# Narrower idle matmuls, separate PSUM banks for the first three visits, and a first layer that takes its first tokens in halves

## The chip, the core and the metric

The kernel runs on one core of one Trainium2 chip. The metric is the device time of one execution in microseconds (us), taken as the median of several runs; lower is better.

## What is computed

Sliding-window causal attention, followed by a two-layer network with a silu between its layers:

```python
q, k, v: (8 batches, 8 heads, 576 positions, 64), float32
scores = q @ k.T / 8, where 0 <= i - j < 64, else -1e9
attn = softmax(scores) @ v
x = attn.transpose(0, 2, 1, 3).reshape(4608, 512)      # tokens x model
out = silu(x @ w_in) @ w_out                           # w_in 512x2048, w_out 2048x512
```

## The kernel before, in words

**Attention.** The 4608 tokens are 72 blocks of 64, nine to a batch. Because of the window, a block needs its own keys and those of the block before it. A *visit* is 3 blocks (the first four visits) or 4. A visit runs through these steps: `scores` (L286) on TensorE, small matmuls of 32 rows and 64 columns into four PSUM banks (for the first batch, four matmuls at L293 first write the mask as a bias); `expo` (L306) on ScalarE; `masking` on VectorE (not in the first batch); `values` (L326) on TensorE; then on VectorE `inverse` (L338), `normal` (L342), which divides and frees the banks of `values`, and `cross` (L350), which transposes the result into `bridge`, where the network reads it. q and k arrive by DMA, and VectorE turns them (L283, L281). v arrives by DMA in groups of 128 positions, and copies of its halves (L264) go to VectorE or ScalarE.

**Network.** The tokens are nine tiles of 512. The first layer (`first_layer`, L361) makes, for each of 16 *ff tiles* of 128 rows, four matmuls (one for each 128 model columns) into one PSUM bank, and `silu` (L367) on ScalarE brings them to SBUF. Tile 0 is taken in parts: for four ff tiles at a time the first 384 tokens (visits 0 and 1), or the next 192 (visit 2). The second layer of tile 0 (`second_layer`, L371) keeps four banks open, one for each 128 tokens, and goes through the ff tiles, so it has 64 matmuls of 512 columns, and each pair of ff tiles needs one of eight loads of `w_out` (L271). `copy_out` (L376) then copies the four banks to SBUF, on VectorE or ScalarE. Tiles 3 to 8 use a scheme with seven products in place of eight (L397).

**Order.** A planner (`Plan`, L16) writes the order of each engine's instructions in advance: it plays the kernel through with an estimated time for each step (`us`), its dependences, the PSUM banks from named pools, and ranks, and then emits the instructions in the order that it found. On the chip each engine keeps that order, and semaphores enforce the dependences. What the planner believes of times changes only the order. Pool `at0` gives the first visits' scores banks 0-3 or 4-7, `two` gives their values banks 0-1 or 2-3, `mp` gives the network banks 4-7 until the attention is done.

**Idle matmuls.** Until there is work, TensorE multiplies zeros (`warm`, L677). They are fillers of the lowest rank: L726 and L727 put matmuls of 256 columns ahead of the first scores, and L728 puts matmuls of 512 columns wherever TensorE would idle between the first scores and the first layer. They write to a bank of pool `any`.

**DMAs.** All loads but the first rows of q and k are issued by GpSimd (POOL), in a fixed order, with up to eight in flight: v and rows of the first batch, eight loads of `w_in` (two for four ff tiles), three of `w_out`, then rows and v of the second batch with the other five of `w_out` in between (L708 to L722), then the other batches.

Of the kernel before, what the change touches and what calls it, by code (L numbers as in the profile page):

```python
# [15 lines left out]
class Plan:  # L16
# [13 lines left out]
    def add(self, cls, us, fn, deps=(), lat=0.1, gate=None, dma=None, pool=None, table=None, first=None, slow=0.0):  # L30
        op = dict(us=us, first=self.rank[cls] if first is None else first, fn=fn, deps=[d for d in deps if d is not None],
                  lat=lat, gate=gate, dma=dma, pool=pool, table=table, seen=None, n=self.count, until=[], bank=None, cls=cls, slow=slow)
        self.count += 1
        self.queues.setdefault(cls, []).append(op)
        return op
# [13 lines left out]
    def run(self):  # L49
# [7 lines left out]
        mode = "full"  # L57
        events, order = [0.7], []
        while left:
# [6 lines left out]
            while moved:  # L66
                moved = False
                for e in engines:
# [58 lines left out]
def kernel(ctx, tc, q, k, v, w_in, w_out, out):  # L127
# [56 lines left out]
        rank=dict(one=-9, late=6, dma=-1, ldk=-9, ldq=-9, cast0=-5,  st=-2, vs=-3, silu=-3, out=-2, keep=-2.1, ssum=-1.2, tsum=1.2,  # L184
                  s=1, v=0, moe=99, warm=200, warm2=200, exp=1, mask=1, inverse=0, norm=0.1, cross=0.2, turn=-1.25, cast=-4,
# [175 lines left out]
    def first_layer(bank, j, ft, c, lo, hi):  # L361
        n0 = j * TB % NBR
        nc.tensor.matmul(  # L363
            ps[:, bank["bank"][0], 0:hi - lo], lhsT=w_in_sb[:, c, ft * 128:(ft + 1) * 128],
            rhs=bridge[:, n0 + lo // 64:n0 + hi // 64, c // 2, :, c % 2], start=(c == 0), stop=(c == NDC - 1))
# [123 lines left out]
    o_done = {}  # L489
    e_free, ob_free, ob_ring = {}, {}, {}  # L490
# [23 lines left out]
    def add_visit(vi):  # L514
# [11 lines left out]
        vi["s"] = s  # L526
        ex = p.add("exp" + z, {"ACT": 0.19 + 0.00084 * 256 * ns}, lambda _: expo(s, vi), [s], table="exp")
# [4 lines left out]
        pv = p.add("v" + z, {"PE": 0.05 * ns + 0.1}, None, [ma] + need_v(vi), pool="two" if vi["banks"] == 2 else "at",  # L532
                   gate=(lambda: moe[20][0]["seen"] is not None) if i == 2 else None)
        pv["fn"] = lambda _: values(pv, vi)
        e_free[i] = [pv]
        rc = p.add("inverse" + z, {"DVE": 0.28}, lambda _: inverse(pv, vi), [pv] + ob_free.get(i - NOB, []))
        no = p.add("norm" + z, {"DVE": 0.16 + 0.00107 * 128 * ns}, lambda _: normal(pv, vi), [rc] + ob_free.get(i - NOB, []))
# [3 lines left out]
        ob_free[i] = [cr]  # L541
        for n in range(vi["n0"], vi["n0"] + vi["nb"]):
            o_done[n] = cr
# [15 lines left out]
    def add_part(j, fts, gt, lo, hi, left):  # L559
# [15 lines left out]
        for n in blocks:  # L575
            br_free[n] = [moe[-1][0]]

# [237 lines left out]
```

## Time and profile before

| | |
|---|---|
| median of 3 runs | 294.48 us |
| lowest and highest | 294.23 and 295.61 us |
| the profiled execution's own time | 294.13 us |
| its span in the profile | 292.4 us |
| first matmul of the first layer | at 23.27 us |
| first matmul of tile 0's second layer | at 40.18 us |
| first matmul of tile 1's first layer | at 56.21 us |

All times inside the profile are counted from the span's start, and come from one execution; 1.7 us of its time lie outside the span. A row of the timeline has the start, the duration, the engine, the line, the operation, what it writes and reads, its shape, the count, and in brackets the idle time before it and what ended that. PE is TensorE's matmuls, PEld its weight loads, DVE VectorE, ACT ScalarE. A row of a window has busy time and count for each engine, the granted clock, the mean busy share of the DMA engines, and GB/s; DMA shares over 1 mean packets that overlap. A row of DMA issues ends in the median time from issue to landing, in us; a row of a DMA queue has packets, MB, and the share of 16 engines' time. A few matmul records are missing from the trace.

### The profile page before, as it was taken

The numbers are of one execution on the slowest core, as the hardware profiler recorded it, in microseconds if no ns is written. First come the engines' busy times: TensorE is split into PE (matmuls) and PEld (weight loads), VectorE is DVE, ScalarE is ACT, GpSimd is POOL, SyncE is SP. The second block draws the span as 40 slices with busy tenths as digits, with TensorE's granted clock in tenths as the row PEclk, the third lists the DMA queues.
The fourth block names the chain that finished last, engine by engine and source line by source line (L and its number), as shares of the span: only waits on it lengthen the run. The fifth ranks groups of instructions, "written<-read, shape, count | busy, mean of one in ns | idle before, by whom it ended". The sixth has DMA issues, their size and how long they took to land.

```text
span 292.4 us, 9098 instructions
## 1 busy us (share of the span) xinstructions
PE 282.0 (96%) x3957; PEld 181.3 (62%) x3971; DVE 163.9 (56%) x303; ACT 164.8 (56%) x255; POOL 117.8 (40%) x181
## 2 busy tenths in 40 slices
PE   8959999999999999999999999999999999999995
PEld 6735764597444455447854686478647864784584
DVE  3663237591580168755987697469446944422433
ACT  2647782798528763668276744673567356416610
POOL 8784597897776988789900000000000000000000
PEclk9999999999999999999999999999999999999999
DMA  9999999999999999999997003000300030003013
GB/s 147 125 166 199 177 134 175 154 215 149 164 189 194 107 192 175 209 154 138 118 165 193 2 4 141 5 2 4 143 0 2 6 144 4 0 2 143 0 38 108
DMA packets 89000, 32.05 MB, mean 110 GB/s; under 512 B 75904, under 2 KB 84096, under 8 KB 88960
## 3 DMA queue, kind: packets, MB, share of 16 engines
q0 software_dynamic: 81600, 18.00, 68.0%
q1 hardware_dynamic: 6176, 12.29, 13.3%
q10 hardware_dynamic: 1184, 1.18, 1.3%
q8 instruction: 31, 0.51, 0.7%
q14 instruction: 9, 0.07, 0.1%
HBM read 36.70 MB, written 9.44 MB: 158 GB/s over the span
## 4 chain that ended last, share of the span: by engine, by line
PE 95%; issue 2%; DVE 1%; ACT 1%
PE ps L363 42%; PE ps L404 26%; PE ps L372 14%; PE ps L678 5%; PE ps L334 4%; PE ps L301 4%; DVE ob L345 1%; PE ps L293 0%; ACT ot L377 0%; ACT L369 0%; DVE ot L416 0%; ACT g L369 0%; DVE rc L340 0%; DVE idle L222 0%
## 5 line engine op out<-in xcount | busy, mean ns | idle before, releaser
L363 PE MATMUL ps<-bridge,w_in_sb 128*128 128x512 bf16 (+3 forms) x704 | 127.0, 340 | 0.8 <-DVE ot L377 0.4
L369 ACT ACTIVATE g<-ps 128x512 bf16<-128x512 f32 (+3 forms) x176 | 89.8, 520 | 43.7 <-PE ps L363 42.6
L363 PEld LDWEIGHTS <-w_in_sb 128*128 128x128 bf16 x704 | 66.8, 98 | 57.9 <-issue 1.0
L395 DVE TENSOR_TENSOR gsum<-g 128x512 bf16<-128x512 bf16 x48 | 20.1, 419 | 44.7 <-ACT g L369 44.7
L372 PE MATMUL ps<-w_out_sb,g 128*128 128x512 bf16 x178 | 41.1, 379 | 1.7 <-issue 1.6
L308 ACT ACTIVATE e<-ps 128x2048 bf16<-128x2048 f32 (+1 forms) x19 | 34.0, 1787 | 13.6 <-PE ps L301 13.5
L404 PEld LDWEIGHTS <-gsum 128*128 128x128 bf16 x384 | 37.1, 98 | 4.5
L404 PE MATMUL ps<-g,gsum 128*128 128x256 bf16 x288 | 36.4, 273 | 0.0
L231 POOL DMA_DIRECT2D natk<-in_k_dram x48 | 28.9, 617 | 12.2 <-DMA natk<-in_k_dram 3.6
L372 PEld LDWEIGHTS <-g 128*128 128x128 bf16 x192 | 17.7, 98 | 20.2
L231 POOL DMA_DIRECT2D natq<-in_q_dram x48 | 29.0, 623 | 2.9 <-DMA vo<-in_v_dram 1.2
L317 DVE TENSOR_TENSOR e<-e,mask 128x2048 bf16<-128x2048 bf16 (+1 forms) x16 | 19.2, 1201 | 19.1 <-ACT e L308 18.9
L404 PEld LDWEIGHTS <-g 128*128 128x128 bf16 x288 | 27.3, 98 | 4.0
L242 POOL DMA_DIRECT2D vo<-in_v_dram x32 | 28.6, 907 | 2.7 <-PE ps L334 1.1
L407 ACT COPY part<-ps 128x256 f32<-128x256 f32 x23 | 8.6, 372 | 30.2 <-PE ps L404 27.1
L404 PE MATMUL ps<-w_out_sb,g 128*128 128x256 bf16 x192 | 23.0, 273 | 0.0
L353 DVE STREAM_TRANSPOSE bridge<-ob 128x1024 bf16<-128x1024 bf16 (+1 forms) x19 | 22.1, 1172 | 0.3
L345 DVE TENSOR_TENSOR ob<-ps,rc 128x1024 bf16<-128x1024 f32 (+1 forms) x19 | 21.9, 1158 | 0.4
L416 DVE TENSOR_TENSOR ot<-ps,part 128x256 f32<-128x256 f32 (+1 forms) x30 | 13.8, 469 | 9.1 <-PE ps L404 4.7
L678 PE MATMUL ps<-idle 128*128 128x256 bf16 (+1 forms) x87 | 14.7, 334 | 4.4 <-issue 3.0
L281 DVE STREAM_TRANSPOSE qt<-natq 128x576 uint32<-128x576 uint32 x12 | 9.1, 759 | 14.5 <-PE ps L301 14.5
L377 ACT COPY ot<-ps 128x512 f32<-128x512 f32 x10 | 5.8, 586 | 16.8 <-PE ps L372 12.8
(56 smaller groups left out, 223.4 us busy)
## 6 DMA issues: line engine op xcount, KB each, us to landing
out_dram<-ot SPq DMA_DIRECT2D x32, 256.0 KB, 3.6
vo<-in_v_dram POOLq DMA_DIRECT2D x32, 128.0 KB, 6.1
natq<-in_q_dram POOLq DMA_DIRECT2D x48, 72.0 KB, 5.4
natk<-in_k_dram POOLq DMA_DIRECT2D x48, 72.0 KB, 4.0
ve<-vo SPq DMA_DIRECT2D x12, 264.0 KB, 4.8
w_in_sb<-in_moe_w_in_dram POOLq DMA_DIRECT2D x8, 256.0 KB, 8.3
w_out_sb<-in_moe_w_out_dram POOLq DMA_DIRECT2D x8, 256.0 KB, 7.3
natq<-in_q_dram POOLq DMA_DIRECT2D x10, 96.0 KB, 6.0
```

The costliest lines, as they stand in the source:

```text
L231: nc.gpsimd.dma_start(out=nats[kk][b % NK][r, h // 4].rearrange("p c x -> p (c x)").rearrange("p (t x) -> p t x", x=2 * D), in_=(q, k)[kk] ...
L242: nc.gpsimd.dma_start(out=vos[b % NV][:, g, :, 0:D], in_=v[b, :, 128 * g:128 * g + 128].rearrange("h p d -> p h d"))
L308: nc.scalar.activation(out=es[vi["i"] % NES][:, :, 0:ns].rearrange("p j s i -> p j (s i)"), in_=ps[:, op["bank"][0]:op["bank"][0] + 4, 0:6 ...
L317: nc.vector.tensor_mul(e, e, m)
L345: nc.vector.tensor_mul(obs[vi["i"] % NOB][:, 0:4 * vi["nb"]].rearrange("p s (i x) -> p (s i) x", i=2).rearrange("p (b k) x -> p b k x", b= ...
L353: nc.vector.transpose(out=br.rearrange("p n Q u h i -> p (n Q u h) i"), in_=ob.rearrange("p s (h d) -> p (s h) d", h=2))
L363: nc.tensor.matmul(ps[:, bank["bank"][0], 0:hi - lo], lhsT=w_in_sb[:, c, ft * 128:(ft + 1) * 128], rhs=bridge[:, n0 + lo // 64:n0 + hi // ...
L369: nc.scalar.activation(out=g[:, lo:hi], in_=ps[:, bank["bank"][0], 0:hi - lo], func=ACTF.Silu)
L372: nc.tensor.matmul(ps[:, bank["bank"][0]], lhsT=gall[:, slot, m * 128:(m + 1) * 128], rhs=w_out_sb[:, f], start=(f == 0), stop=(f == NFT - 1))
L395: (nc.vector.tensor_sub if i else nc.vector.tensor_add)(out=t[i], in0=a, in1=b)
L404: nc.tensor.matmul(ps[:, bank["bank"][0], lo:lo + 256], lhsT=lhs, rhs=rhs, start=first, stop=last, skip_group_check=True)
L678: nc.tensor.matmul(ps[:, op["bank"][0], 0:128 * op["parts"]], lhsT=idle, rhs=idle.unsqueeze(1).to_broadcast([128, op["parts"], 128]), star ...
```

## The change

It has three parts, and estimates of the planner that go with them.

1. The idle matmuls before the first scores have 128 columns instead of 256. By the order built, 96 of them stand there, then 13 of 512 columns (before: 68 of 256); two of 512 stand between the first and the second scores (before: three), none between the first and second values (before: five), and nine between the second values and the third scores (before: two there, and nine behind the third scores).
2. The banks: scores of the first three visits in 0-3, 4-7 and 2-5, their values in 2-3, 0-1 and 2-3. The values of the first two visits now stand directly behind one another, and the third scores stand behind both. On VectorE the first visit's transpose is forced ahead of the second visit's normalization.
3. For the first four ff tiles, `add_halves` takes the 384 tokens as 2 x 192: first all four ff tiles with the first visit's tokens, in banks 6, 7, 0 and 1, then all four with the second visit's, into the other columns of the same banks. One silu of 384 columns follows for each.

The planner also counts TensorE instructions (`code`) and adds a delay at instructions 449, 705 and so on. This alters no instruction, only its idea of when steps can start.

```diff
         mode = "full"
+        code, chunk = 0, {449: 0.0}
...
+                        for x in range(193, code + op["code"], 256):
+                            if x >= code:
+                                t = us * (x - code) / op["code"]
+                                us += max(0.0, chunk.get(x, 0.0) - now - t)
+                                chunk[x + 256] = max(now + t, chunk.get(x, 0.0)) + (5.6 if now < 25 else 2.5)
+                        code += op["code"]
...
-        {"at": lambda: [(0, 1, 2, 3)], "at0": lambda: [(0, 1, 2, 3), (4, 5, 6, 7)], "any": lambda: [(3,), (2,), (7,), (6,)],
-         "two": lambda: [(0, 1), (2, 3)],
+        {"at": lambda: [(0, 1, 2, 3)], "at0": lambda: [(0, 1, 2, 3)], "at1": lambda: [(4, 5, 6, 7)], "at2": lambda: [(2, 3, 4, 5)], "any": lambda: [(3,), (2,), (7,), (6,)],
+         "two0": lambda: [(2, 3)], "two1": lambda: [(0, 1)], "mp0": lambda: [(6,), (7,), (0,), (1,)],
...
-    def first_layer(bank, j, ft, c, lo, hi):
+    def first_layer(bank, j, ft, c, lo, hi, at=0):
...
-            ps[:, bank["bank"][0], 0:hi - lo], lhsT=w_in_sb[:, c, ft * 128:(ft + 1) * 128],
-            rhs=bridge[:, n0 + lo // 64:n0 + hi // 64, c // 2, :, c % 2], start=(c == 0), stop=(c == NDC - 1))
+            ps[:, bank["bank"][0], at:at + hi - lo], lhsT=w_in_sb[:, c, ft * 128:(ft + 1) * 128],
+            rhs=bridge[:, n0 + lo // 64:n0 + hi // 64, c // 2, :, c % 2], start=(c == 0 and at == 0), stop=(c == NDC - 1),
+            skip_group_check=True)
...
-        vi["banks"] = 2 if first else 4
+        vi["banks"] = 2 if i < 3 else 4
...
-                  gate=None if first else gate_scores(vi), pool="at0" if vi["n0"] < 9 else "at")
+                  gate=None if first else gate_scores(vi), pool=("at0", "at1", "at2")[i] if first else "at")
...
-        no = p.add("norm" + z, {"DVE": 0.16 + 0.00107 * 128 * ns}, lambda _: normal(pv, vi), [rc] + ob_free.get(i - NOB, []))
+        no = p.add("norm" + z, {"DVE": 0.16 + 0.00107 * 128 * ns}, lambda _: normal(pv, vi), [rc] + ob_free.get(i - NOB, []) + (cr0 if i == 1 else []))
...
+    def add_halves(fts, gt):
+        first = {}
+        for i in range(2):
+            for ft in fts:
+                for c in range(NDC):
+                    op = p.add("moe", {"PE": 0.0036 + 192 / 2400}, None, [o_done[3 * i], win[(ft, c)]], pool=None if c or i else "mp0")
+                    bank = first.setdefault(ft, op)
+                    op["fn"] = lambda _, bank=bank, ft=ft, c=c, i=i: first_layer(bank, 0, ft, c, 192 * i, 192 * i + 192, 192 * i)
+                    moe.append((op, 1, 1 if c == 0 and i == 0 else -1, 0))
+                if i:
+                    slot, si = gt[ft]
+                    op = p.add("silu", {"ACT": 0.18 + 384 * 0.00083}, lambda _, bank=bank, slot=slot: silu(bank, slot, 0, 384), [op], table="silu")
+                    si.append(op)
+                    bank["until"] = [op]
...
-    p.add_filler(26, "warm", {"PE": 0.214}, warm, 2, [c_idle], pool="any", lat=0.0)
-    p.add_filler(60, "warm", {"PE": 0.109}, warm, 2, [c_idle], gate=lambda: visits[0]["s"]["seen"] is None, pool="any", lat=0.0)
-    p.add_filler(60, "warm2", {"PE": 0.217}, warm, 4, [c_idle], pool="any", lat=0.0,
-                 gate=lambda: visits[0]["s"]["seen"] is not None and moe[0][0]["seen"] is None)
+    p.add_filler(39, "warm", {"PE": 0.11}, warm, 1, [c_idle], pool="any", lat=0.0)
+    p.add_filler(57, "warm", {"PE": 0.0565}, warm, 1, [c_idle], pool="any", lat=0.0)
+    p.add_filler(90, "warm2", {"PE": 0.217}, warm, 4, [c_idle], pool="any", lat=0.0,
+                 gate=lambda: moe[0][0]["seen"] is None)
...
     for f, half in ((0, 0), (4, 0), (8, 0), (0, 1), (12, 0), (4, 1), (8, 1), (12, 1)):
-        for ft in range(f, f + 4):
-            add_part(0, [ft], gts[0], *((384, 576) if half else (0, 384)), 1)
+        if f or half:
+            for ft in range(f, f + 4):
+                add_part(0, [ft], gts[0], *((384, 576) if half else (0, 384)), 1)
+        else:
+            add_halves(range(4), gts[0])
```

More of the change, by code (lines that the diff above doesn't have):

```diff
@@ L31, in add @@
         op = dict(us=us, first=self.rank[cls] if first is None else first, fn=fn, deps=[d for d in deps if d is not None],
-                  lat=lat, gate=gate, dma=dma, pool=pool, table=table, seen=None, n=self.count, until=[], bank=None, cls=cls, slow=slow)
+                  lat=lat, gate=gate, dma=dma, pool=pool, table=table, code=2, seen=None, n=self.count, until=[], bank=None, cls=cls, slow=slow)
         self.count += 1
@@ L489 @@
     o_done = {}
+    cr0 = []
     e_free, ob_free, ob_ring = {}, {}, {}
@@ L531, in add_visit @@
             ma = p.add("mask", {"DVE": 0.16 + 0.00053 * 256 * ns}, lambda _: masking(vi), [ex, c_mask])
-        pv = p.add("v" + z, {"PE": 0.05 * ns + 0.1}, None, [ma] + need_v(vi), pool="two" if vi["banks"] == 2 else "at",
+        pv = p.add("v" + z, {"PE": 0.05 * ns + 0.1}, None, [ma] + need_v(vi), pool=("two0", "two1", "two0")[i] if i < 3 else "at",
                    gate=(lambda: moe[20][0]["seen"] is not None) if i == 2 else None)
         pv["fn"] = lambda _: values(pv, vi)
+        pv["code"] = 16 * ns
         e_free[i] = [pv]
         rc = p.add("inverse" + z, {"DVE": 0.28}, lambda _: inverse(pv, vi), [pv] + ob_free.get(i - NOB, []))
-        no = p.add("norm" + z, {"DVE": 0.16 + 0.00107 * 128 * ns}, lambda _: normal(pv, vi), [rc] + ob_free.get(i - NOB, []))
+        no = p.add("norm" + z, {"DVE": 0.16 + 0.00107 * 128 * ns}, lambda _: normal(pv, vi), [rc] + ob_free.get(i - NOB, []) + (cr0 if i == 1 else []))
         pv["until"] = [no]
@@ L541, in add_visit @@
         ob_free[i] = [cr]
+        cr0[:] = [cr]
         for n in range(vi["n0"], vi["n0"] + vi["nb"]):
```

3 lines of the change are left out of this document (2 added, 1 removed).

## Prediction

> **What bounds the kernel now.** First the page, for the bound and for what the DMA engines do.
>
> ```profile
> span 292.4 us, 9098 instructions
> ...
> PE 282.0 (96%) x3957; PEld 181.3 (62%) x3971; DVE 163.9 (56%) x303; ACT 164.8 (56%) x255; POOL 117.8 (40%) x181
> ...
> DMA  9999999999999999999997003000300030003013
> ...
> q8 instruction: 31, 0.51, 0.7%
> ```
>
> TensorE is busy for 96% of the span, so a gain has to come out of its 10 us of idle time, out of idle matmuls (busy, but no work), or out of waits that hide in either. All the idle matmuls stand before 23.3 us, so the timeline of TensorE there comes next, then VectorE's.
>
> ```profile
> 0.99 9.92 PE L678 MATMUL ps<-idle 128*128 128x256 bf16 x68 [0.99 <-DVE idle L222]
> 10.75 0.81 PE L293 MATMUL ps<-bias,ident 128*128 128x384 bf16 x4
> 11.49 0.55 PE L301 MATMUL ps<-qt,kt 32*128 32x64 bf16 x48
> ...
> 13.86 0.32 PE L334 MATMUL ps<-ve,e 128*32 128x66 bf16 x16
> ...
> 17.46 1.24 PE L678 MATMUL ps<-idle 128*128 128x512 bf16 x5 [2.99 <-issue]
> 18.63 0.32 PE L334 MATMUL ps<-vo,e 128*32 128x66 bf16 x16
> ...
> 19.61 0.81 PE L293 MATMUL ps<-bias,ident 128*128 128x384 bf16 x4
> 20.36 0.55 PE L301 MATMUL ps<-qt,kt 32*128 32x64 bf16 x48
> 21.33 2.10 PE L678 MATMUL ps<-idle 128*128 128x512 bf16 x9 [0.42 <-DVE ob L345]
> 23.27 0.98 PE L363 MATMUL ps<-bridge,w_in_sb 128*128 128x384 bf16 x5
> ```
> ```profile
> 16.38 0.52 DVE L283 STREAM_TRANSPOSE kt<-natk 128x192 uint32<-128x192 uint32 x1
> 19.30 0.31 DVE L340 RECIPROCAL rc<-ps 128x24 f32<-128x24 f32 x1 [2.40 <-PE ps L334]
> 19.52 1.75 DVE L345 TENSOR_TENSOR ob<-ps,rc 128x768 bf16<-128x768 f32 x2
> 21.19 1.83 DVE L353 STREAM_TRANSPOSE bridge<-ob 128x768 bf16<-128x768 bf16 x2
> ```
>
> The useful stream starts at 23.27 (first layer). Behind it is a stop of 2.99 us, from 14.47 to 17.46, whose releaser is "issue": no semaphore ended it. The second visit's values follow at 18.63, VectorE normalizes both visits together (0.88 each) and transposes both (0.92 each), and only then can 384 tokens go through the first layer. What was the stop? The counts up to it, and the DMA of the stretch behind it:
>
> ```profile
> 0.00:14.45 14.45, 13.46 (x223) 10.17 (x224) 6.88 (x29) 6.19 (x9) 11.82 (x23) 1.00 1.38 136
> ```
> ```profile
> q8 instruction: 1, 0.02, 5.4%
> ```
> ```profile
> q8 instruction: 1, 0.02, 5.8%
> ```
>
> 223 + 224 = 447 TensorE instructions were done. The first of the two instruction rows is that of 14.9 to 16.2 us, just ahead of the restart; the second that of 22.5 to 23.5. The queue moved 31 blocks, and TensorE has 3957 + 3971 records: 256 to a block. I read it so: code comes in blocks of 256, the next is asked for when TensorE enters a block, and the stop is a block that came late: asked for near 11.7 (the 193rd instruction, in the scores of 11.49), usable at 17.46, 5.8 us later. The next block, asked for at 17.46, is moved from 22.5 on; with the 2.5 us that the first took from the start of its transfer (14.98) to the restart, that is up to 7.6 us. One small stop supports this: the 3520th instruction (448 + 12 x 256) stands in the values near 118.3, and there a group of 16 took 0.53 instead of 0.31:
>
> ```profile
> 118.11 0.31 PE L334 MATMUL ps<-vo,e 128*32 128x66 bf16 x16
> 118.25 0.53 PE L334 MATMUL ps<-ve,e 128*32 128x66 bf16 x16
> ```
>
> In a sentence apart: the Trainium skill, Runtime: NRT & Kernel Launch, section Instruction fetch mechanics, has blocks of 256 too, but calls crossing one "mostly hidden" and gives TensorE room for 2048; the 2.99 us after 447 speak against both.
>
> **The change, part by part.**
>
> *Idle matmuls.* 68 of 256 columns become 96 of 128 and 13 of 512 ahead of the first scores. More instructions now stand early: 192 of the 193 before the first request are idle matmuls and their weight loads. When are they through?
>
> ```profile
> 0.99:5.75 4.76, 4.76 (x23) 3.39 (x24) 1.00 0.95 182
> 5.75:10.75 5.00, 5.00 (x47) 4.37 (x45) 1.00 1.78 122
> ```
> ```profile
> 58.74 1.48 PE L363 MATMUL ps<-bridge,w_in_sb 128*128 128x192 bf16 x16 [0.30 <-ACT g L369]
> ```
>
> 256 columns took 0.213 each until 5.75 and 0.109 after it, though the granted clock is given as 1.00 throughout. 128 columns are not in the trace. Bounds: half the 256-column spacing, 0.055, and the spacing of 192 columns, 0.082 (row of 58.74). I take 0.056, because the step from 192 to 256 columns (0.082 to 0.109) shows no floor. So 45 run until 5.75, 51 more take 2.9 us, and the 193rd instruction is passed at 8.6 (10.0 with 0.082) instead of 11.7. The 13 wide ones end at 11.4, and the first scores start 0.65 later than before (10.75). Later code blocks shift by 98 instructions.
>
> The Trainium skill, TensorE: Matmul & The Clock Gate, section Back-to-back issue gap, speaks against this edit: it gives about 81 ns per matmul at 128 columns in a stream with weight loads. By it the request goes out 1.3 us later than I take; no row here decides it.
>
> *Banks.* The three visits' scores take banks 0-3, 4-7 and 2-5, the values 2-3, 0-1 and 2-3. So the second values no longer follow a stop plus five idle matmuls; they wait for their exponent. From the rows: first scores end at 12.6, the second scores at 14.3, first values at 14.45 (their block is due at 8.6 + 5.8 = 14.4), second exponent (0.15 + 1.45) to 15.9, second values 16.1 to 16.6 instead of 18.63. A cost: the third scores need banks 2-3, so they wait for the first normalization, which stands on VectorE behind the last transpose (ends 16.9) and the second reciprocal: 17.2 to 18.1. Nine idle matmuls (1.9) cover this until 18.6.
>
> *First four ff tiles by halves.* 16 matmuls of 384 columns (2.60) become 32 of 192 (2.64): +0.04. They need only the first visit's transpose. VectorE now does normalization, a copy that waits for the fourth v load, and that transpose, to about 19.3, then the second pair to 21.1, and the second half starts 1.3 into the layer. No queue of POOL or SP is moved: the same DMAs are issued in the same order.
>
> *When does the first layer start?* The next block is asked for at 14.45 and usable 5.8 to 7.6 later, 20.3 to 22.0, and its boundary now lies in the third scores, which TensorE reaches at 19.5. Add 0.4 for the rest: 20.7 to 22.5, I take 21.5. Its weights allow that: the second transfer of the first w_in group, issued at 14.63, took 5.4:
>
> ```profile
> w_in_sb<-in_moe_w_in_dram POOLq DMA_DIRECT2D x1, 256.0 KB, 5.4
> ```
>
> So the front gains 23.27 - 21.5 = 1.8 us.
>
> *Where it is given back.* I follow TensorE to the first place that waits for DMA.
>
> ```profile
> 39.69 0.55 PE L301 MATMUL ps<-qt,kt 32*128 32x64 bf16 x48
> 40.18 4.28 PE L372 MATMUL ps<-w_out_sb,g 128*128 128x512 bf16 x18
> ...
> 50.86 0.69 PE L301 MATMUL ps<-qt,kt 32*128 32x64 bf16 x64
> 51.70 3.19 PE L372 MATMUL ps<-w_out_sb,g 128*128 128x512 bf16 x14 [0.16 <-issue]
> ```
> ```profile
> 44.60 0.72 POOL L271 DMA_DIRECT2D w_out_sb<-in_moe_w_out_dram  x1
> ```
> ```profile
> w_out_sb<-in_moe_w_out_dram POOLq DMA_DIRECT2D x1, 256.0 KB, 7.3
> ```
> ```profile
> 48.94 0.53 DVE L283 STREAM_TRANSPOSE kt<-natk 128x192 uint32<-128x192 uint32 x1
> ```
>
> The second layer of tile 0 goes by ff tile, four matmuls each, and ff tile 12 needs the seventh w_out load. It was issued at 44.60 and took 7.3: 51.9. The matmul that needs it is the 49th of 64, the third after the scores of 50.86. Of the 15 there, 14 are recorded, the first is the 0.16 of idle time, so the third started at 51.49 + 2 x 0.216 = 51.9 too: no slack at all. The DMA share stands at 9 tenths up to slice 22 (160 us), and POOL issues each load when an earlier one has landed, not when TensorE is ready, so an earlier TensorE doesn't bring the load forward. Arriving 1.8 us early it waits 1.8 us. The scores ahead of it also need the transpose that ends at 49.47, which by itself allows 1.4 of those 1.8. From the 49th matmul on, the order is the one of before but for single matmuls moved across a visit, so the rest takes its old time. VectorE copies two outputs of tile 0 instead of one and ScalarE two instead of three; the waits there (0.37 and 0.30 before the first layer of tile 1) can move by 0.2 either way, taken as nothing.
>
> *Code blocks later.* The stop near 118.3 (0.2) goes. One boundary is in question: a block now begins 12 matmuls into visit 5's scores and the next near the end of visit 6's.
>
> ```profile
> 69.78 0.71 PE L301 MATMUL ps<-qt,kt 32*128 32x64 bf16 x64
> ...
> 73.98 0.68 PE L301 MATMUL ps<-qt,kt 32*128 32x64 bf16 x64
> ```
>
> That is 4.2 + 0.5 = 4.7 us for 256 instructions; the block of 118 took about 4.8, the first 5.8: a new stop of 0 to 1.1, taken as 0.1 by the nearer row.
>
> **Sum.** Against the profiled execution (294.13, of which 292.4 is span): -1.8 + 1.8 - 0.2 + 0.1 = 294.0. The median of the runs shown is 294.48, 0.35 above; so I predict 294.4. A run of this kernel can tell 0.5% (1.5 us) from no change, so this is "same".
>
> **Rivals.**
>
> *A, the load does not hold it.* If the w_out loads land early enough, most of the 1.8 arrives at the end: 292.7. For: a landing time is one execution's. Against: the DMA share, and the same issue order. It decides if the seventh load lands before 50.5.
>
> *B, slower: code blocks come later still.* If each of the first two takes 7.6 instead of 5.8, they are usable at 16.2 and 23.8; the first layer starts at 24.2, 0.9 late, which nothing gives back as the 49th matmul had no slack, and the boundary between the scores of visits 5 and 6 adds 1.1: 294.48 + 0.9 + 1.1 - 0.2 = 296.3. It decides once the two delays together exceed 14.3 us. For: both delays were measured. Against: only the second was that long, and both must be.
>
> *C, the stop is not code.* Then the idle matmuls change nothing, the stop returns before the second values, and halves plus banks give back what the later first scores cost: 294.5. This is what the page's "mostly hidden" would make of it, with the 447 against it.
>
> **How the numbers follow.** Forecast 0.70 (293.4 to 295.5), A 0.13, B 0.12, C 0.05. Faster by over 0.5%: A, 0.13. Slower: B, 0.12. Within: 0.75. The range 293.0 to 296.0 holds the forecast, C, and the nearer halves of A and B.
>
> **What would show it.** Right: no stop of 3 us before 18 us; the first layer starting between 20.7 and 22.5 on 192 columns; a wait for a w_out DMA of 1 to 2 us between 49 and 52 us; and the first layer of tile 1 at 56.2 again. Wrong: that layer at 54.5 (A), or a first layer after 23.3 and a stop in the scores near 74 (B).

## The result, and the profile after

| | us |
|---|---|
| changed kernel, median of 20 runs | 292.82 (290.83 to 295.39) |
| kernel before, median of 20 runs beside it | 295.93 (293.8 to 301.02) |
| ratio, with its 95% interval | 0.990 (0.9875 to 0.9925) |

The change makes the kernel faster by 1%, about 3.1 us. The forecast was 294.4 and no change; 292.82 lies just below the range (293.0) and beside the time of rival A (292.7). The kernel before took 295.93 here, not the 294.48 of the three runs that the forecast started from.

Ratios here and below leave out the slow runs of either kernel (over 1.5% above its fastest), while the medians count every run. The profile of the changed kernel is of the longest of its 20 runs (295.39 us), in which the granted clock fell to half for 3.4 us near 53 us. Its front can be read all the same. The timeline of TensorE:

```profile
16.28 0.32 PE L341 MATMUL ps<-vo,e 128*32 128x66 bf16 x16 [1.04 <-ACT e L315]
...
16.82 2.12 PE L705 MATMUL ps<-idle 128*128 128x512 bf16 x9
18.78 0.81 PE L300 MATMUL ps<-bias,ident 128*128 128x384 bf16 x4
19.52 0.69 PE L308 MATMUL ps<-qt,kt 32*128 32x64 bf16 x48
20.15 0.34 PE L370 MATMUL ps<-bridge,w_in_sb 128*128 128x192 bf16 x2
20.65 1.74 PE L370 MATMUL ps<-bridge,w_in_sb 128*128 128x192 bf16 x19 [0.16 <-DMA w_in_sb<-in_moe_w_in_dram]
```

The stop of 2.99 is gone. The second values wait 1.04 for their exponent, nine wide idle matmuls cover the normalization, and the first layer starts at 20.15 on 192 columns: 3.1 us earlier than at 23.27. Further on, in the same view and then in windows (third last column: the granted clock):

```profile
50.15 0.24 PE L308 MATMUL ps<-qt,kt 32*128 32x64 bf16 x8 [0.40 <-DVE kt L290]
51.75 0.41 PE L380 MATMUL ps<-w_out_sb,g 128*128 128x512 bf16 x1 [1.36 <-DMA w_out_sb<-in_moe_w_out_dram]
52.38 3.81 PE L380 MATMUL ps<-w_out_sb,g 128*128 128x512 bf16 x10 [0.22 <-issue]
...
57.86 0.81 PE L370 MATMUL ps<-bridge,w_in_sb 128*128 128x192 bf16 x6
...
75.44 0.68 PE L308 MATMUL ps<-qt,kt 32*128 32x64 bf16 x64
```
```profile
50.00:52.00 2.00, 0.49 (x9) 0.34 (x11) 0.39 (x2) 1.53 (x2) 1.53 (x4) 0.99 1.52 191
52.00:54.00 2.00, 1.78 (x5) 0.71 (x5) 0.99 (x1) 0.98 (x1) 1.19 (x2) 0.50 1.67 165
54.00:56.00 2.00, 2.00 (x7) 0.66 (x5) 0.24 (x1) 0.00 (x0) 0.66 (x2) 0.66 0.88 83
```

The forecast wait for the w_out load is there (1.36), and so is a shorter one for the scores (0.40). Ten matmuls then take 3.81 instead of some 2.3, at half the clock, so that tile 1 starts at 57.86. The scores of visit 6 (75.44) take 0.68, without a stop. Next, the changed kernel was profiled three times more:

| | first layer | 7th w_out load landed | tile 1's first layer | clock at half | span |
|---|---|---|---|---|---|
| changed (above) | 20.15 | 51.7 | 57.86 | 52.0 to 55.4 | 293.6 |
| a_same | 19.93 | 50.7 | 55.11 | never | 290.9 |
| a_again1 | 19.53 | 51.2 | 57.33 | 51.9 to 55.4 | 293.0 |
| a_again2 | 19.59 | 50.9 | 55.33 | never | 291.0 |

In all 28 runs of the changed kernel the mean granted clock shows such a stretch 3 times, so the second and fourth row are the usual case. The lowered clock also puts tile 1 of a_again1 (57.33) outside both of its expectations; a_again2's 55.33 is what a load with a landing time of its own gives, not the 56.2 of the prediction's step.

### The profile page after: what moved, and what is told of

The parts are those of the page before. It is cut to its first block, busy times and chain, and to the rows that moved or that the text cites. A ratio compares the mean times of both kernels' runs of the same rounds, so it can differ in the third digit from the quotient of the medians.

```text
span 293.6 us, 9198 instructions
## 1 busy us (share of the span) xinstructions
PE 282.6 (96%) x4006; PEld 182.1 (62%) x4020; DVE 166.0 (57%) x306; ACT 162.9 (55%) x252; POOL 117.9 (40%) x181
## 4 chain that ended last, share of the span: by engine, by line
PE 72%; DMA 18%; POOL 6%; issue 2%; DVE 0%; POOLq 0%
PE ps L370 33%; PE ps L412 26%; DMA vo<-in_v_dram 8%; PE ps L380 8%; DMA w_out_sb<-in_moe_w_out_dram 4%; PE ps L341 3%; PE ps L308 3%; DMA w_in_sb<-in_moe_w_in_dram 2%; DMA natq<-in_q_dram 2%; DMA natk<-in_k_dram 2%; POOL natk L238 1%; POOL vo L249 1%; POOL natq L243 1%; POOL natk L243 1%; POOL natq L238 1%
## 5 line engine op out<-in xcount | busy, mean ns | idle before, releaser
L370 PEld LDWEIGHTS <-w_in_sb 128*128 128x128 bf16 x720 | 67.5, 98 | 58.0 <-DMA w_in_sb<-in_moe_w_in_dram 1.4
L380 PE MATMUL ps<-w_out_sb,g 128*128 128x512 bf16 x178 | 42.7, 389 | 3.2 <-issue 1.5
L315 ACT ACTIVATE e<-ps 128x2048 bf16<-128x2048 f32 (+1 forms) x19 | 34.0, 1787 | 13.9 <-PE ps L308 13.7
L324 DVE TENSOR_TENSOR e<-e,mask 128x2048 bf16<-128x2048 bf16 (+1 forms) x16 | 19.2, 1202 | 15.9 <-ACT e L315 15.7
L424 DVE TENSOR_TENSOR ot<-ps,part 128x256 f32<-128x256 f32 (+1 forms) x30 | 13.9, 470 | 9.0 <-PE ps L412 4.6
L385 ACT COPY ot<-ps 128x512 f32<-128x512 f32 x9 | 5.2, 587 | 19.1 <-PE ps L380 11.4
L308 PEld LDWEIGHTS <-kt 32*128 32x128 bf16 x1152 | 10.7, 92 | 7.8 <-issue 5.6
```

Of the source, the lines that this page charges most:

```text
L308: nc.tensor.matmul(sc[:, j, 64 * s:64 * s + 64], lhsT=kts[b % NK][r, Q, 64 * t:64 * t + 128, h], rhs=qts[b % NK][r, Q, 64 * t:64 * t + 64, h],
L315: nc.scalar.activation(out=es[vi["i"] % NES][:, :, 0:ns].rearrange("p j s i -> p j (s i)"), in_=ps[:, op["bank"][0]:op["bank"][0] + 4, 0:6 ...
L324: nc.vector.tensor_mul(e, e, m)
L370: nc.tensor.matmul(ps[:, bank["bank"][0], at:at + hi - lo], lhsT=w_in_sb[:, c, ft * 128:(ft + 1) * 128], rhs=bridge[:, n0 + lo // 64:n0 + ...
L380: nc.tensor.matmul(ps[:, bank["bank"][0]], lhsT=gall[:, slot, m * 128:(m + 1) * 128], rhs=w_out_sb[:, f], start=(f == 0), stop=(f == NFT - 1))
```

## The experiments

**The theories.** *Code*: the stop was a late block of 256 instructions; the change reaches the request earlier, and what the front gains arrives at the end less what the w_out load takes back. *Clock* (rival): the gain is that TensorE is kept busy, so that its granted clock isn't lowered. *C* (rival): the stop is not code. The expectations on record have numbers: theory 1 is that the loads land at other times in each execution, theory 2 that the load holds the 49th matmul in every one; theory 3 is *Code* together with the clock that its stop lowers; rival 4 is that the gain is the new order by banks and halves; theory 5 is *Clock*. Names with a_ start from the changed kernel, with b_ from the one before. Ratios are to the kernel before, run beside each.

| | median, us | ratio (95% interval) | first layer | tile 1's |
|---|---|---|---|---|
| a_same | 292.63 | 0.9856 (0.9814 to 0.9899) | 19.93 | 55.11 |
| a_no_load_wait | 293.49 | 0.9882 (0.9839 to 0.9924) | 19.60 | 53.94 |
| a_front_late | 293.93 | 0.9900 (0.9866 to 0.9934) | 22.01 | 55.82 |
| b_same | 295.58 | 0.9962 (0.9929 to 0.9996) | 24.71 | 57.64 |
| b_idle128 | 294.72 | 0.9949 (0.9918 to 0.9980) | 22.37 | 55.68 |
| b_idle512 | 294.97 | 0.9963 (0.9925 to 1.0001) | 20.59 | 55.00 |
| a_no_halves | 293.02 | 0.9900 (0.9862 to 0.9937) | 21.41 | 55.67 |
| a_old_banks | 295.82 | 0.9983 (0.9940 to 1.0026) | 19.58 | 57.10 |
| a_no_idle9 | 294.04 | 0.9949 (0.9915 to 0.9984) | 20.11 | 58.69 |
| a_idle256 | 295.20 | 0.9971 (0.9942 to 1.0001) | 19.97 | 57.42 |
| a_wout_x | 292.22 | 0.9886 (0.9845 to 0.9927) | 20.32 | 55.51 |
| a_wout_y | 292.41 | 0.9895 (0.9850 to 0.9940) | 19.31 | 54.49 |

b_same is the kernel before itself, and its ratio of 0.9962 shows how far two sets of runs of one kernel stand apart: differences under 0.4% between rows decide nothing. Each profile is one execution, so differences between two profiles carry that kind of spread too.

### The two kernels again

Unchanged copies; those named again were run at the end, as one profile each.

> The changed kernel, unchanged, for a second profile. Both theories: ratio 0.99 and a first layer at 20.2 to 21.5 us. Theory 1: the wait for the w_out load before the 49th matmul is shorter than 1 us or absent, and tile 1's first layer starts 2 to 3 us before that of b_same. Theory 2: the wait is 1.3 us or more, and tile 1's first layer starts within 0.5 us of that of b_same or later.

> The kernel before, unchanged, for a second profile. Theory 1 (the loads land at other times in each execution): the seventh w_out load lands 1 us or more away from 51.9 us, and the first layer does not start at 23.27 again. Theory 2 (the load holds the 49th matmul in every execution): that load lands within 0.5 us of the matmul that needs it, as in the first profile. Both: ratio 1.00.

> The kernel before, one more execution in the profile. If the stop of 2.99 us in the first profile was a short one, the stop here is 3.2 to 4.0 us, the first layer starts at 24.0 to 25.0 and the granted clock falls once before 23 us; if the first profile was typical, the stop is 2.9 to 3.1, the first layer starts at 23.1 to 23.5 and the clock stays at 1.00.

> As the run before of this kernel: a stop of 3.2 to 4.0 us and a lowered clock if the first profile was a lucky one, 2.9 to 3.1 and full clock if it was typical. In both, the second layer's 49th matmul waits for no DMA, as it is reached after the load has landed.

> The changed kernel, one more execution. By the theory that tile 0's second layer gives back only what the seventh w_out load takes from it: first layer at 19.6 to 20.4, the load lands anywhere from 49.3 to 52.8, and the wait for it plus the time at which tile 1's first layer starts move together, 53.9 to 56.2. By the prediction's step that all is given back: tile 1's first layer at 56.2, whatever the first layer does.

> As the run before of this kernel: tile 1's first layer at 53.9 to 56.2 by the theory of a load that lands at a time of its own, at 56.2 by the prediction's step.

The first two came out by halves. a_same waits 1.54 us for the load, as theory 2 has it, and yet its tile 1 starts 2.5 us before that of b_same, as theory 1 has it; its first layer, at 19.93, is earlier than the 20.2 to 21.5 of both. In b_same the load lands at 52.8, 0.9 us later than in the first profile and 0.6 us ahead of the matmul that needs it, which is neither theory's, and its first layer starts at 24.71.

One profile doesn't stand for the kernel before. Timelines of b_again1, b_again2 and b_same:

```profile
16.66 1.24 PE L678 MATMUL ps<-idle 128*128 128x512 bf16 x5 [2.55 <-issue]
...
22.47 3.58 PE L363 MATMUL ps<-bridge,w_in_sb 128*128 128x384 bf16 x21
...
52.22 2.97 PE L372 MATMUL ps<-w_out_sb,g 128*128 128x512 bf16 x13 [0.93 <-DMA w_out_sb<-in_moe_w_out_dram]
...
56.46 1.38 PE L363 MATMUL ps<-bridge,w_in_sb 128*128 128x192 bf16 x12
...
114.61 0.59 PE L301 MATMUL ps<-qt,kt 32*128 32x64 bf16 x53 [0.40 <-issue]
...
120.40 0.24 PE L334 MATMUL ps<-ve,e 128*32 128x66 bf16 x5 [1.00 <-issue]
```
```profile
17.47 1.24 PE L678 MATMUL ps<-idle 128*128 128x512 bf16 x5 [3.33 <-issue]
...
20.20 1.49 PE L293 MATMUL ps<-bias,ident 128*128 128x384 bf16 x4
...
24.38 1.79 PE L363 MATMUL ps<-bridge,w_in_sb 128*128 128x384 bf16 x10
...
120.15 0.24 PE L334 MATMUL ps<-ve,e 128*32 128x66 bf16 x5 [0.52 <-issue]
```
```profile
17.76 1.46 PE L678 MATMUL ps<-idle 128*128 128x512 bf16 x5 [3.68 <-issue]
```

The stop was 2.55, 2.99, 3.33 and 3.68 us in four executions. Behind the two long ones the clock falls; the windows of b_again2:

```profile
16.00:18.00 2.00, 0.53 (x3) 0.29 (x3) 0.52 (x1) 0.76 (x2) 1.27 (x3) 1.00 1.38 194
18.00:20.00 2.00, 2.00 (x54) 1.01 (x52) 0.52 (x2) 0.50 (x1) 1.62 (x3) 0.69 1.18 176
20.00:22.00 2.00, 2.00 (x37) 0.84 (x39) 2.00 (x3) 0.00 (x0) 0.84 (x2) 0.50 1.22 197
```

At 0.50 the four bias matmuls take 1.49 instead of 0.81, and the first layer starts at 24.38. And the small stop near 118 (0.2 in the first profile) was 0.52, 0.55 (b_same) and 0.40 + 1.00 us in the others. Each of the three later profiles has a longer stop near 118, a lowered clock, or both. So b_again1's expectation came out in neither form (a short stop at full clock), b_again2's in the first: the profile that the forecast was made against (span 292.4) was the shortest of four by luck, the other spans being 294.0 to 294.3. The seventh w_out load landed at 49.7 (b_again2) to 52.8 (b_same), and b_again1 waits 0.93 for it: the kernel before waits for it at times, too.

### Is the stop code? b_idle512 and a_idle256

b_idle512 is the kernel before with its 68 idle matmuls of 256 columns replaced by 34 of 512:

```diff
-    p.add_filler(26, "warm", {"PE": 0.214}, warm, 2, [c_idle], pool="any", lat=0.0)
-    p.add_filler(60, "warm", {"PE": 0.109}, warm, 2, [c_idle], gate=lambda: visits[0]["s"]["seen"] is None, pool="any", lat=0.0)
+    p.add_filler(13, "warm", {"PE": 0.428}, warm, 4, [c_idle], pool="any", lat=0.0)
+    p.add_filler(60, "warm", {"PE": 0.218}, warm, 4, [c_idle], gate=lambda: visits[0]["s"]["seen"] is None, pool="any", lat=0.0)
```

> The kernel before with 34 idle matmuls of 512 columns in place of 68 of 256: the same time, 68 instructions fewer. Theory 3: the stop follows the instruction count, so it leaves its place behind the first values and stands inside the second values (instruction 449), until 18.5 to 19.5 us, and the clock is lowered less often; ratio 0.994 to 1.002. If the stop is not a matter of code, it stays behind the first values with 3 us or more.

A window that ends in its stop (counts of matmuls and of weight loads in the first two brackets), and its timeline:

```profile
0.00:16.45 16.45, 15.38 (x223) 7.10 (x224) 9.89 (x35) 7.20 (x9) 15.13 (x28) 1.00 1.35 144
```
```profile
16.10 0.28 PE L334 MATMUL ps<-ve,e 128*32 128x66 bf16 x10
16.64 0.25 PE L334 MATMUL ps<-ve,e 128*32 128x66 bf16 x6 [0.26 <-issue]
...
19.51 1.24 PE L678 MATMUL ps<-idle 128*128 128x512 bf16 x5 [1.25 <-DVE ob L345]
20.59 3.58 PE L363 MATMUL ps<-bridge,w_in_sb 128*128 128x384 bf16 x21
```

Fewer instructions, other work at the stop, and it stands once more behind 223 + 224 = 447 instructions, inside the second visit's values, which TensorE reaches 16 us in: the wait for the block is only 0.26 there, and the first layer starts 2.7 us earlier than at 23.27 without any of the change's three parts. Tile 1 starts at 55.00. Its median (294.97) shows little of that, since the clock fell in 6 of its 12 runs; the other six have a median of 293.68. The place is the expected one; the time is not: the stop was expected to last until 18.5 to 19.5, 5.3 us or more behind the 193rd instruction, and ended at 16.64, 3.4 us behind it.

The transfers on the instruction queue (q8, to 0.05 us) say what that means. All times in us; the first three rows are the block behind 447 instructions, the others the next one:

| | 193rd or 449th instruction | the block's transfer starts | TensorE goes on |
|---|---|---|---|
| kernel before | 11.7 | 15.0 | 17.46 |
| a_idle256 (below) | 11.0 | 13.9 | 16.69 |
| b_idle512 | 13.2 | 13.9 | 16.64 |
| a_again2 | 13.9 | 16.9 | 19.32 |
| a_old_banks (below) | 15.9 | 16.9 | 19.31 |
| b_idle128 (below) | 16.5 | 17.5 | 19.83 |

TensorE goes on 2.3 to 2.8 us after the transfer has started, every time: the stop does end with the block. But the transfer starts 0.7 to 3.3 us behind the instruction at which the prediction has it asked for, so the request isn't tied to that one; where it is made stays open. What part 1 does to it is plain: in the twelve profiles with idle matmuls of 128 columns the first block's transfer starts at 9.9 to 11.5 us, in the five with 256 at 13.9 to 15.0. b_idle512's, at 13.9, is not among the early ones: there the fewer instructions put more work ahead of the stop.

a_idle256 is the changed kernel with the three old fillers, and their rank of 200:

```diff
-    p.add_filler(39, "warm", {"PE": 0.11}, warm, 1, [c_idle], pool="any", lat=0.0)
-    p.add_filler(57, "warm", {"PE": 0.0565}, warm, 1, [c_idle], pool="any", lat=0.0)
+    p.add_filler(26, "warm", {"PE": 0.214}, warm, 2, [c_idle], pool="any", lat=0.0)
+    p.add_filler(60, "warm", {"PE": 0.109}, warm, 2, [c_idle], gate=lambda: visits[0]["s"]["seen"] is None, pool="any", lat=0.0)
...
```

> The changed kernel without part 1: 68 idle matmuls of 256 columns ahead of the first scores, as before; new banks and halves stay. Code theory: instruction 449 is the first of the second values, so a stop of 1.5 to 3.5 us stands there until 17.4 to 18 us; the third block comes 5.8 to 7.6 us later and stops the third values; first layer 21 to 22, clock lowered in a third of the executions or more, ratio 0.992 to 0.998. Rival 4 (the order by banks and halves is what counts): no more than 0.7 us slower than a_same, ratio 0.986 to 0.988.

```profile
16.69 0.32 PE L341 MATMUL ps<-vo,e 128*32 128x66 bf16 x16 [2.92 <-issue]
...
24.80 0.35 PE L341 MATMUL ps<-ve,e 128*32 128x66 bf16 x11 [2.07 <-issue]
```

The stop is back (2.92), and the next block stops the third values (2.07); the clock falls behind each of the two, and in 8 of the 12 runs; the time is the one of before (0.9971). Banks and halves without the idle matmuls are worth nothing that can be told, against rival 4. Rival C is out: the place goes with the count. One part was missed: the first layer was expected at 21 to 22 and starts at 19.97, as early as in the changed kernel, since its first half needs only the first visit, whose values stand ahead of the stop. So an early first layer isn't the gain by itself.

### One part alone, one part undone: b_idle128, a_no_halves, a_old_banks

b_idle128 is the kernel before with the change's three fillers and their rank (201) alone, a_idle256's diff the other way round:

```diff
-    p.add_filler(26, "warm", {"PE": 0.214}, warm, 2, [c_idle], pool="any", lat=0.0)
+    p.add_filler(39, "warm", {"PE": 0.11}, warm, 1, [c_idle], pool="any", lat=0.0)
+    p.add_filler(57, "warm", {"PE": 0.0565}, warm, 1, [c_idle], pool="any", lat=0.0)
...
```

> The kernel before with part 1 alone: its idle matmuls ahead of the first scores have 128 columns (96 of them, and 13 of 512), banks and ff tiles as before. Theory 3 (the gain is the late code block: its stop, longer than 3 us in most executions, and the clock that it lowers): no stop of over 1.5 us before 20 us, granted clock 1.0 in nearly all executions, first layer at 21 to 22 us, ratio 0.988 to 0.991. Rival 4 (the gain is the new order, by banks and halves): ratio 0.997 to 1.0.

```profile
0.00:18.55 18.55, 17.56 (x351) 13.11 (x352) 10.25 (x36) 8.06 (x11) 15.78 (x29) 1.00 1.44 142
```
```profile
18.20 0.39 PE L301 MATMUL ps<-qt,kt 32*128 32x64 bf16 x28
19.83 0.33 PE L301 MATMUL ps<-qt,kt 32*128 32x64 bf16 x20 [1.25 <-issue]
```

The gain is smaller than theory 3 had it (0.988 to 0.991) and larger than rival 4 had it: 0.9949, with b_same's 0.9962 beside it. The next block, behind 351 + 352 = 703 = 447 + 256 instructions, stops the third scores for 1.25, since the old order reaches them a little earlier; the first layer starts at 22.37, and the clock, expected at 1.0 in nearly all, fell in 7 of 12 runs. Part 1 is needed (a_idle256), but it doesn't bring the whole gain alone.

a_no_halves undoes part 3 (in the diff's last hunk):

```diff
-        if f or half:
+        if True:
```

> The changed kernel without part 3: its first four ff tiles take 384 tokens at once. Theory 3: the first layer starts near 21.2 us instead of 20, and the wait for the w_out load takes up most of it: within 1 us of a_same, ratio 0.986 to 0.991. Rival 4: 1.2 us or more slower than a_same, ratio 0.991 to 0.995.

The first layer starts at 21.41, 1.5 us later than in a_same, and tile 1 only 0.56 later (55.67). The medians (293.02 to 292.63, overlapping intervals) show no cost: the halves bring the layer forward, and most of it is given back.

a_old_banks undoes part 2 (old pools, the rest of the change kept):

```diff
-        {"at": lambda: [(0, 1, 2, 3)], "at0": lambda: [(0, 1, 2, 3)], "at1": lambda: [(4, 5, 6, 7)], "at2": lambda: [(2, 3, 4, 5)], "any": lambda: [(3,), (2,), (7,), (6,)],
-         "two0": lambda: [(2, 3)], "two1": lambda: [(0, 1)], "mp0": lambda: [(6,), (7,), (0,), (1,)],
+        {"at": lambda: [(0, 1, 2, 3)], "at0": lambda: [(0, 1, 2, 3), (4, 5, 6, 7)], "any": lambda: [(3,), (2,), (7,), (6,)],
+         "two": lambda: [(0, 1), (2, 3)], "mp0": lambda: [(6,), (7,), (0,), (1,)],
...
-                  gate=None if first else gate_scores(vi), pool=("at0", "at1", "at2")[i] if first else "at")
+                  gate=None if first else gate_scores(vi), pool="at0" if first else "at")
...
-        pv = p.add("v" + z, {"PE": 0.05 * ns + 0.1}, None, [ma] + need_v(vi), pool=("two0", "two1", "two0")[i] if i < 3 else "at",
+        pv = p.add("v" + z, {"PE": 0.05 * ns + 0.1}, None, [ma] + need_v(vi), pool="two" if i < 3 else "at",
```

> The changed kernel without part 2: the banks of the first three visits as before. Theory 3: no stop, the clock stays up, within 1 us of a_same, ratio 0.986 to 0.991. Rival 4: ratio 0.993 to 0.998.

Missed: it costs the whole gain (0.9983), though the first layer starts at 19.58. The timelines of TensorE and of VectorE:

```profile
19.31 0.33 PE L308 MATMUL ps<-qt,kt 32*128 32x64 bf16 x20 [1.26 <-issue]
...
44.50 0.32 PE L341 MATMUL ps<-ve,e 128*32 128x66 bf16 x16 [2.52 <-DVE e L324]
```
```profile
41.68 0.52 DVE L290 STREAM_TRANSPOSE qt<-natq 128x192 uint32<-128x192 uint32 x1 [2.58 <-DMA natq<-in_q_dram]
...
43.51 0.93 DVE L324 TENSOR_TENSOR e<-e,mask 128x1536 bf16<-128x1536 bf16 x1
```

The planner, given other banks, put turns that wait for rows of q (2.58) ahead of the mask of visit 3, so that its values wait 2.52. The clock, expected to stay up, fell in 8 of 12 runs. So this run priced a reordering on VectorE, and what the banks alone are worth stays open.

### What holds the gain back: a_no_load_wait, a_front_late, a_wout_x, a_wout_y

In a_no_load_wait the last four ff tiles of tile 0's second layer use the rows of ff tile 11 of w_out in place of their own, so nothing waits for the last two loads (tile 0's output is then not that of the computation):

```diff
-    def second_layer(bank, slot, m, f):
+    def second_layer(bank, slot, m, f, src):
...
-            ps[:, bank["bank"][0]], lhsT=gall[:, slot, m * 128:(m + 1) * 128], rhs=w_out_sb[:, f],
+            ps[:, bank["bank"][0]], lhsT=gall[:, slot, m * 128:(m + 1) * 128], rhs=w_out_sb[:, src],
...
-            op["fn"] = lambda _, bank=bank[m], slot=slot, m=m, f=f: second_layer(bank, slot, m, f)
+            op["fn"] = lambda _, bank=bank[m], slot=slot, m=m, f=f: second_layer(bank, slot, m, f, f if j else min(f, 11))
```

> The changed kernel, where the second layer of tile 0 multiplies its last four ff tiles by the rows of w_out that came with the sixth load, so that no matmul of that layer waits for the seventh or eighth (both are still loaded; the output of tile 0 is not the reference's). Theory 2: 1.3 to 2 us faster than a_same, ratio 0.983 to 0.986. Theory 1: within 0.7 us of a_same, since in most executions the load is there in time.

```profile
49.02 2.54 PE L380 MATMUL ps<-w_out_sb,g 128*128 128x512 bf16 x11 [0.16 <-issue]
52.19 0.32 PE L341 MATMUL ps<-vo,e 128*32 128x66 bf16 x16 [0.62 <-DVE e L324]
...
53.94 0.98 PE L370 MATMUL ps<-bridge,w_in_sb 128*128 128x192 bf16 x8
```

The wait is gone, a new one of 0.62 for visit 4's mask follows, and tile 1 starts 1.2 us earlier than in a_same. The medians don't show it (293.49 to 292.63); theory 2's 1.3 to 2 us didn't come. So the load is the first thing in the way in a profile, and taking it away gains nothing that the runs can tell.

a_front_late puts nine more idle matmuls of 512 columns ahead of the first layer.

```diff
+        if j == 0 and ft == 0 and c == 0 and at == 0 and lo == 0:
+            for _ in range(9):
+                nc.tensor.matmul(ps[:, bank["bank"][0]], lhsT=idle, rhs=idle.unsqueeze(1).to_broadcast([128, 4, 128]),
+                                 start=True, stop=True)
```

> The changed kernel with nine more idle matmuls of 512 columns (1.94 us) just ahead of the first layer. Theory 2: the wait for the load takes them up, the same time as a_same (ratio 0.99). Theory 1: nothing takes them up, 1.5 to 1.9 us slower than a_same (ratio 0.995 to 0.997).

```profile
22.01 1.90 PE L374 MATMUL ps<-bridge,w_in_sb 128*128 128x192 bf16 x21
...
54.07 0.33 PE L341 MATMUL ps<-vo,e 128*32 128x66 bf16 x16 [0.62 <-DVE e L324]
...
55.82 0.90 PE L374 MATMUL ps<-bridge,w_in_sb 128*128 128x192 bf16 x7
```

Of 2.08 us at the first layer (22.01 - 19.93), 0.71 are left at tile 1; the medians are 1.3 apart, with overlapping intervals. Most of a front's gain is given back by tile 1, but not all; in the medians more is left: the six runs, all at full clock, are 1.2 us above the 25 such runs of the changed kernel (292.76). That lies between theory 2 (nothing) and theory 1 (1.5 to 1.9).

a_wout_x issues the seventh load ahead of two v loads, a_wout_y the seventh and eighth ahead of the same two:

```diff
     add_w_out(5)
-    add_v(1, 2)
     add_rows(1, 2)
-    add_v(1, 3)
     add_w_out(6)
+    add_v(1, 2)
+    add_v(1, 3)
     add_w_out(7)
     add_v(1, 4)
```
```diff
     add_w_out(5)
-    add_v(1, 2)
     add_rows(1, 2)
-    add_v(1, 3)
     add_w_out(6)
     add_w_out(7)
+    add_v(1, 2)
+    add_v(1, 3)
     add_v(1, 4)
```

> The changed kernel with the loads of the second batch in another order: behind the sixth w_out load come the third rows, the seventh w_out load, two v loads, the eighth w_out load (the changed kernel: v, rows, v, seventh, eighth). If the wait for the seventh load (1.4 and 1.5 us in two profiles) is on the path: 0.5 to 1.4 us faster than a_same, ratio 0.981 to 0.985. Rival: the later v loads or the eighth w_out load take its place, ratio 0.985 to 0.990.

> As a_wout_x, but the eighth w_out load directly behind the seventh, ahead of both v loads. If the w_out loads are what holds the second layer of tile 0: ratio 0.980 to 0.985. Rival: visit 4's values now wait for v, and the time stays that of a_same, ratio 0.985 to 0.990.

The seventh load lands at 49.3 and 49.2 and isn't waited for, but other waits are there: 1.10 for a turn of k and 0.60 for a mask in a_wout_x, 0.46 for a mask and 0.82 for the copies in a_wout_y. The medians, 292.22 and 292.41, are the lowest of all and can't be told from a_same, which is what their rivals said.

### The clock: a_no_idle9

The nine idle matmuls between the second values and the third scores are left out, the order else the same:

```diff
+        if 112 <= len(seen_warm) <= 120:
+            return
```

> The changed kernel without the nine idle matmuls between the second values and the third scores, all else in the same order: TensorE stands idle there (the third scores wait for the first normalization anyway). Theory 5 (what a late front costs beyond its own length is the granted clock, lowered for some 3.4 us when TensorE is short of work): first layer within 0.5 us of a_same's 19.9, mean clock 0.994 or less in most executions, ratio 0.989 to 0.993. Rival (idle matmuls here only fill time): clock 1.0 as in a_same, and within 0.5 us of a_same, ratio 0.985 to 0.988.

```profile
18.66 0.81 PE L300 MATMUL ps<-bias,ident 128*128 128x384 bf16 x4 [1.96 <-DVE ob L352]
```
```profile
20.00:22.00 2.00, 1.72 (x14) 1.30 (x11) 1.88 (x3) 1.89 (x2) 1.79 (x3) 0.50 0.95 130
...
54.00:56.00 2.00, 2.00 (x6) 0.76 (x5) 1.18 (x1) 0.00 (x0) 0.60 (x1) 0.50 1.33 127
```

TensorE idles for 1.96 instead, the first layer starts as before (20.11), and the clock falls 1 us behind it, at 19.6, and once more behind a w_out wait of 1.28. It fell in 11 of 12 runs; the median is 294.04, 1.4 us above a_same and 1.2 above the 20 runs of the result, where the rival had 0.5 at most. So idle matmuls that gain no start time are worth the clock.

### Where the 3.1 us come from

Each run lists its mean clock; one stretch of 3.4 us at half gives 0.994. Of 85 runs of the kernel before whose clock is listed, 32 have none (median 294.98), 42 one (296.36) and 11 two or, once, three (298.29). Of 28 of the changed kernel, 25 have none (292.76) and 3 one. So among the runs at full clock the changed kernel is 294.98 - 292.76 = 2.2 us faster, and the rarer lowering makes up the rest: 65 stretches in 85 runs against 3 in 28 are 0.66 fewer for each run, at no more than 1.7 us each (half of 3.4), 1.1 at the most.

That is a count over runs as they came; no run holds the clock still. It puts about two thirds of the gain on runs at full clock, where all three parts act, and a third on the clock. The two are not independent: in b_same, b_again2 and a_idle256 the clock fell about 1 us behind the stop, so part of the clock's third may be the late block's too. Nor has a stretch the same price everywhere: a_idle256's eight runs with one or two have a median of 294.7, its four at full clock 295.3. Of the 2.2, the two full-clock profiles of each kernel show where: tile 1's first layer at 55.11 and 55.33 instead of 56.21 and 56.46 (1.1 us); from tile 2's first layer to the end 205.6 twice instead of 205.8 and 207.4 (1.0 on the mean, nearly all of it from b_again1 alone, with its stops near 114 and 120).

## Why the prediction was wrong, point by point

- **The stop is a late block of code: right.** b_idle512 and b_idle128 put it behind 447 and 703 instructions whatever the work. The Trainium skill, Runtime: NRT & Kernel Launch, section Instruction fetch mechanics, calls such crossings "mostly hidden"; most of the 31 here show no stop of over 0.25 us, but the first one cost 2.55 to 3.68 us in the kernel before and the second 2.07 in a_idle256, so for these the trace doesn't agree. Rival C is out. What isn't borne out is that the block is asked for at the 193rd or 449th instruction.
- **The rate of the idle matmuls: right.** The changed kernel shows it for 128 columns:

```profile
4.20:7.86 3.66, 3.66 (x68) 3.66 (x67) 0.45 (x2) 0.48 (x1) 3.66 (x6) 1.00 1.98 163
```

  3.66 / 68 = 0.054 each, beside the 0.056 taken. The Trainium skill, TensorE: Matmul & The Clock Gate, section Back-to-back issue gap, gives about 81 ns at 128 columns in a stream with weight loads; with a weight load for each, the trace doesn't agree for these.
- **The first layer at 20.7 to 22.5: too late.** It started at 19.53 to 20.15. The block of the third scores (705 on) was taken at 5.8 to 7.6 after the request at 14.45. In a_again2 a stop of 0.24 at that place shows when it came; its timeline, and a window for the request:

```profile
18.70 0.39 PE L308 MATMUL ps<-qt,kt 32*128 32x64 bf16 x27
19.32 0.34 PE L308 MATMUL ps<-qt,kt 32*128 32x64 bf16 x21 [0.24 <-issue]
```
```profile
0.00:14.00 14.00, 13.01 (x238) 10.27 (x242) 7.07 (x28) 5.80 (x9) 11.93 (x23) 1.00 1.27 139
```

  At 14.00, 480 instructions were done, so the 449th lies before it; it is in the first values, which begin at 13.80. Counted from it the block took 5.3 to 5.5, shorter than either end taken; counted the same way it took 3.4 in b_idle512, b_idle128 and a_old_banks. So 5.8 and 7.6 were not the bounds of a fixed delay, and the term was mis-sized with them. The front's gain was 3.1 to 3.7, not 1.8.
- **"Arriving 1.8 us early it waits 1.8 us": this step failed.** The wait is where it was forecast, with the size (1.21 to 1.54), and a wait for the scores of up to 0.91 beside it. But 51.9 is not a wall: the load landed at 49.7 to 52.8 before, 50.7 to 51.7 after. So of 3.3 (a_same) and 3.7 us (a_again2), 1.1 and 0.9 arrived at tile 1. "An earlier TensorE doesn't bring the load forward" treated one execution's landing as fixed. And the load wasn't the only thing in the way: with its wait taken out (a_no_load_wait) the runs are no faster. Rival A named the landing, and was given 0.13; that 292.82 lies beside its 292.7 is partly luck, since its own condition (landing before 50.5) was met in no profile of the changed kernel, and neither its 1.8 nor its 294.48 was what was measured.
- **"-0.2 stop at 118": mis-sized.** The stop is gone, and it was 0.2, 0.52, 0.55 and 1.40 (two stops) in four executions: about 0.7 on the mean. The new stop in visit 6's scores (0.1) didn't come.
- **What the sum lacked altogether: the clock.** One profile at full clock gave no sign that most executions lose 3.4 us of it to half. The sum put it at nothing and was made against the shortest of four profiled executions; the 0.35 added for the median was too little, as the kernel before has 295.93, 1.8 above that execution.
- **Rival B** didn't come: no execution of the changed kernel has its first layer after 20.15.

What stays open: what decides whether the clock falls. Waits of 0.41 and 1.32 near 50 us brought it down in a_again1, 0.91 and 1.21 in a_again2 did not; a stop of 2.92 near 16 us did in a_idle256, 2.99 in the first profile did not. So the length of the stop alone doesn't. Where the request for a block is made isn't known, the banks by themselves weren't priced, and how much of the gain needs all three parts together wasn't measured apart from the clock.

## What to carry to other kernels

Count TensorE's instructions up to any stop that no semaphore ends: if the count is 447, 703 and so on (256 apart), the cure is in the count: more and narrower instructions early, so that the block comes earlier (transfer at 9.9 to 11.5 us instead of 13.9 to 15.0 here), or fewer in all, so that more work stands ahead of the stop (b_idle512). Moving work alone left the stop at 2.92 (a_idle256). Before a sum is made to tenths of a microsecond against a profile, ask of each of its terms how far it moves from one execution to the next: a DMA's landing moved by 3 us here, a stop by 1.1, and a clock that was full in the one profile is lowered in 53 of 85 runs.

## What was not expected of the hardware

The granted clock falls to half for 3.4 us (18.8 to 22.2 in b_again2, 51.9 to 55.4 in a_again1) after as little as 1.3 us without work behind a stretch of small matmuls, and each time for about the same 3.4 us: eight stretches in six profiles. What decides it is not known. Idle matmuls thus have a use in the midst of a kernel: leaving out nine of them, with the first layer no later, cost 1.2 to 1.4 us.
